# Gate loop and GEGLU kernel: residuals added by accumulating DMAs, later v loads on GpSimd's queue, one more group turned by DMA, and a new written-out order

## The chip, the cores and the metric

The kernel runs on one core of one Trainium2 chip. The metric is the device time of one execution in microseconds (us). Three runs of the kernel before took 276.53, 273.31 and 271.00 us, so its median is 273.31 us.

## The reference, cut to what matters

Part one is a complex gated linear recurrence over 768 steps for 4 batches and 8 heads of width 48. Part two is a gated feed-forward block with a gated residual over the 3072 resulting tokens of width 384.

```python
mag = np.sqrt(a_re * a_re + a_im * a_im)
scale = np.minimum(mag, 0.999) / (mag + 1e-06)
for t in range(S):
    new_re = ar * S_re - ai * S_im
    new_im = ar * S_im + ai * S_re
    S_re, S_im = new_re + k_t (outer) v_t, new_im
    y[t] = q_t @ S_re
...
g = x @ w_gate
gelu = 0.5 * g * (1.0 + erf(g * inv_sqrt2))
ffn_out = gelu * (x @ w_val) @ w_out
return x + 1.0 / (1.0 + np.exp(-(x @ w_res))) * ffn_out
```

## The kernel before, in words

The 768 steps are cut into chunks of 128. Two chunks (c = 0 and 1) of one batch make a group p; there are 12 groups, p = 4 s + b for the third s of the sequence and the batch b. A group is computed as masked attention inside a chunk, plus a state G that is carried from third to third.

Every piece of work is a named step. `Steps.add` (line 360) records it with its engine, what it reads and what it writes; the string `ORDER` (line 260) lists all steps, and the last loop of the kernel (lines 926 to 931) emits them one after the other. Each engine, and each DMA queue, therefore gets its own steps in the order of that list, and it goes through them strictly in that order: a step that has to wait holds up everything behind it on that engine. The number after a colon picks the buffer of a tile (`Y5.1:2` puts the output x of group 5, chunk 1 in x buffer 2 of 9). The words `log`, `trig` and `gelu` are loads of an activation table on ScalarE (line 929), which is on ACT. The table `eo` in `PARAMS` (line 64) says which engine does a step that more than one engine could do.

The steps of a group p, in the order of the data:

- Loads on SP's queue, 192 KB each: `Lar`, `Lai`, `Lq`, `Lk` (line 516), `Lvf` (line 880). The v data land as float32 in `vf` (2 buffers) and are cast to bfloat16 by `VC` (lines 882 and 883) on POOL, ACT or DVE.
- Gates (lines 518 to 648): squares `SQI` and `SQR`, `ADD`, logarithms and exponentials `LNR`, `EXR`, `LM`, the angle `TH` and `ATN`, all over 128x768 float32. Sums over time on PE: `CSL` (line 588) for the magnitude, followed by `EX` and `EI` on ACT; `CST` (lines 621 and 622) for the angle, followed by `OFF` and `FR`, `ABS`, `SIN` and `COS`.
- The angle of chunk 0 has to be carried to chunk 1. There are two ways. For a group in the list `cma`, one more matrix product with a constant (line 621) adds the sum over chunk 0 inside `CST p.1`. For a group that is not in the list, `CRA p` scales the last row of chunk 0 (line 670), and `CDA p`, an accumulating DMA from POOL's queue (line 675), adds it to the first row of `ai` of chunk 1; only then can `CST p.1` run. `CRB` and `CDB` are the same from third to third.
- The decay of the state over a third: the small DMAs `DR`, `DS`, `DE`, `DI`, `DT` from POOL's queue, `ML` and `ME` on ACT, `MM` and `MN`, then `EN` (line 755, scales G) and `EB` (line 760, casts it).
- Products (lines 684 to 702): `QE`, `KE`, `QR`, `KR` on DVE write padded q and k tiles. From group `turn` on, `QT` and `KT` (line 700) turn them with DMA transposes on SP's queue. For the groups before it, four `TP` steps (line 727, eight transposes each, on PE) and four `CP` copies (line 732, on DVE or ACT) do that.
- Attention (lines 704 to 799): `AT` on PE, `AM` (mask) on DVE, `DK`, `MI`, `ED` for the state, `Y` on PE, and `X`, the cast of the output to the bfloat16 tile x, on ACT or DVE. There is one PSUM tile for y.

The feed-forward block works on 8 units. Units 0 to 3 are one group each (256 tokens), units 4 to 7 are two groups each (512 tokens, four chunks jj = 0 to 3). x is turned by PE (`XT`, `XC`) for groups 0 to 4 and by DMA (`XD`, line 809) from group 5 on. Then come `GP` and `VP` (line 828, PE), `GE` (gelu, ACT), `HM` (line 839, DVE), `RP` (line 843, PE) and `SG` (ACT), `OP` (line 853, 12 products, PE), `OT` (line 858, DVE), the residual and the store `ST` (line 868, SP's queue). The residual is one of:

- `RX` (line 865): POOL or DVE adds x to the output tile before the store. All 24 chunks do this in the kernel before.
- `AX` (line 871): the tile is stored without x, and a DMA on POOL's queue then adds x to the stored rows in DRAM. It reads x and the stored output, so it waits until `ST` has landed, and the buffer of x is free only after it.

The weights (line 894) come as 12 casting DMAs on POOL's queue: `Wg0` to `Wg3`, `Wv0` to `Wv3`, `Wr`, `Wo0` to `Wo2`. `HOLDW` and `HOLDO` are one-element copies on POOL that wait for a load of `ai`, so that what stands behind them on POOL starts later.

The lines that choose between the ways:

```python
if p >= TURN:                                              # QT, KT  (699)
both = p in PARAMS["cma"] and c == 1                       # (612)
if p in PARAMS["vhw"]:                                     # Lvf + VC  (878)
    ...
else:
    st.add("LV%d.%d" % (p, c), "POOL", lambda c=c: nc.gpsimd.dma_start(out=st["v", p][:, c], in_=rows(v, p, c)), ...)   # (886)
rese = PARAMS["rese"][min(u, len(PARAMS["rese"]) - 1)] if u < NU - 1 else PARAMS["resl"]   # (861)
if rese == "DMA":
    st.add("AX%d.%d" % (u, jj), "POOL", lambda t0=t0, pc=(p, c): nc.gpsimd.dma_start(
        out=out[t0:t0 + 128, :], in_=st["x", pc], accum_op=OP.add),
        r=[("x", (p, c)), ("out", (u, jj))], w=[("out", (u, jj))])                          # (871)
```

Of the kernel before, what the change touches and what calls it, by code (L numbers as in the profile page):

```python
# [18 lines left out]
 'turn': 5,  # L19
# [39 lines left out]
 'rese': ['POOL'],  # L59
 'resl': 'POOL',  # L60
 'vhw': [0, 1, 2, 3, 4, 5, 6, 7, 8, 9, 10, 11],
 'cma': [4, 5, 6, 7, 8, 9, 10, 11],
# [50 lines left out]
        'MM7': 'DVE',  # L113
        'MM8': 'DVE',
        'MM9': 'DVE',
        'MN10': 'POOL',
        'MN11': 'DVE',
        'MN4': 'DVE',
# [4 lines left out]
        'MN9': 'DVE',  # L123
# [64 lines left out]
        'SQR10': 'DVE',  # L188
        'SQR11': 'ACT',
        'SQR2': 'ACT',  # L190
# [3 lines left out]
        'SQR6': 'ACT',  # L194
# [66 lines left out]
Lar0.1:0 log LNR0.1:0 SQR0.1 Lai0.1:0 SQI0.1:0 ADD0.1 LM0.1 EXR0.1 TH0.1 Lar0.0 Lai0.0 LNR0.0 EXR0.0 SQI0.0 TH0.0 trig  # L261
ATN0.0 CST0.0:0 SQR0.0 ATN0.1 CSL0.1:10 CST0.1:2 Lai1.1:1 Lar1.1:1 Lai3.0:2 Lai4.1:3 Lai1.0 ADD0.0 SQI1:1 log LM0.0
EI0.1 CSL0.0:3 Lar1.0 SQR1 ADD1 LM1 OFF0.1 FR0.1 ABS0.1 LNR1 EX0.1 EXR1 Lk0.0:0 TH1 Lai3.1 Lvf0.1:0 Lai5.1:4 EX0.0
EI0.0 OFF0.0 VC0.1:0 DE0:0 CRB0 HOLDO Lar3.1:2 Lk0.1 trig ATN1 FR0.0 SIN0.0:0 SIN0.1 SQI3:2 ABS0.0 COS0.0 CSL1.1:211
CST1.0:1 KE0.1 CSL1.0:3 KE0.0 CST1.1:0 Lq0.0:0 Lar3.0 SQR3 ADD3 COS0.1 KR0.0 log LNR3 KR0.1 Lar4.1:3 EX1.1 Lvf0.0:1
Lai4.0 SQI4:3 OFF1.0 OFF1.1 VC0.0 FR1.1 QE0.0 EX1.0 EXR3 DE1:1 DK0.0 QR0.0 Lar4.0 Lq1.0:1 Lai2.0:5 Lvf1.1:0 Lq0.1
EI1.0 FR1.0 ABS1 SQR4 CRB1 Lai5.0 Lar2.1:0 Lai2.1 TP0.0.1:00 TP0.0.0:11 Lq1.1 EI1.1 CP0.0.0 Lar2.0 AT0.0.0:00 LM3
QE0.1 TH3 QR0.1 AM0.0.0 ADD4 CP0.0.1 DR4:0 Lk1.0:1 QE1 TP0.1.0:31 AT0.0.1:11 trig SIN1:1 SQI2:0 ATN3 SQR2 COS1
TP0.1.1:20 AM0.0.1 Y0.0:0 CP0.1.1 Lk1.1 ADD2 log LM2 CSL3.1:100 AT0.1.1:00 CST3.1:0 CSL3.0:2 QR1 KE1 CP0.1.0
AT0.1.0:11 AM0.1.1 AM0.1.0 EI3.1 EX3.0 EI3.0 CSL2.1:311 CST3.0:2 OFF3.1 LNR4 EX3.1 MI0:0 FR3.1 X0.0 Lar5.1:1 Lvf1.0:1  # L270
Lar5.0 Wg0 Wg2 Wv3 Wg3 EI2.1 Wg1 Wv0 KR1 EX2.1 Y0.1:1 X0.1 XT0.1:10 TP1.0.0:00 XC0.1 EXR4 OFF3.0 FR3.0 VC1.0:1 Wr SQR5
XT0.0:3 CP1.0.0 XC0.0 CRB3 TP1.0.1:11 SQI5:1 LNR2 EXR2 CP1.0.1 ABS3 Wo2 Wv1 GP0.5:2 trig COS3:0 DK0.1 ED0 ADD5 VC1.1
Lk2.0:2 GP0.0:0 AT1.0.0:00 gelu GE0.0 HOLDW Lq2.0:2 GP0.2:3 Lar7.1:2 AT1.0.1:11 GP0.4:1 GE0.2 GE0.4 GE0.5 AM1.0.0
TP1.1.0:00 CP1.1.0 RP0.0:3 GP0.3:1 RP0.1:0 TH4 Lq3.0:3 Lk2.1 GP0.1:2 SG0.0 DK1.0 SG0.1 Lq2.1 Wo0 TP1.1.1:31 Lvf2.0:1
Lq3.1 GE0.1 AM1.0.1 TH2 DE2:2 GE0.3 CP1.1.1 Lk3.0:3 VP0.0:0 Y1.0:2 X1.0 AT1.1.0:00 AM1.1.0 MI1:1 VP0.5:2 CSL2.0:1 trig
ATN2 HM0.5 HM0.0 CST2.1:3 AT1.1.1:11 AM1.1.1 OFF2.1 log LNR5 EX2.0 EXR5 EI2.0 FR2.1 CST2.0:2 Y1.1:3 DK1.1 X1.1 LM4
trig ATN4 XT1.0:01 XC1.0 Wv2 OFF2.0 FR2.0 TH5 ABS2 SIN2:1 SIN3 COS2 VP0.4:3 VP0.2:0 VP0.3:1 VP0.1:2 HM0.2 HM0.3 HM0.1
HM0.4 DS4.0:0 DR5:1 Wo1 KE2 DS4.1 Lai6.0:0 KR2 QE2 ATN5 DS5.0:1 QR2 XT1.1:0 CSL4.0:111 DS5.1 OP0.0.0:2 OT0.0:0 log ML5
EI4.0 OP0.1.0:3 EX4.0 XC1.1 OT0.1:1 CRB2 TP2.0.0:10 Lai6.1 GP1.2:0 GP1.1:2 CP2.0.0 TP2.0.1:31 AT2.0.0:00 QE3 RX0.0 QR3
DI4 ED1 AM2.0.0 DE3:3 CDB0 VC2.0:2 CDB1 gelu GE1.2 GE1.1 Lvf2.1:0 Lar9.1:3 Lk3.1 VC2.1 Lai7.0:1 GP1.0:1 RP1.0:0  # L280
TP2.1.1:20 CP2.0.1 DT4.0:0 AT2.0.1:11 GP1.5:3 GE1.0 SQI6:2 SG1.0 GE1.5 CP2.1.1 AM2.0.1 DK2.0 VP1.5:1 GP1.3:0 HM1.5
MI2:0 KE3 RP1.1:2 DT4.1 RX0.1 GP1.4:3 Y2.0:4 Lvf5.0:1 VP1.0:1 X2.0 HM1.0 KR3 SG1.1 GE1.4 GE1.3 CST4.1:2 TP2.1.0:31
CSL4.1:0 VC5.0:3 Lar6.1:0 CP2.1.0 Lai11.1:2 Lar7.0 Lar6.0 CST4.0:1 AT2.1.1:00 log LM5 CSL5.0:300 EX4.1 ML4 OFF4.1
EI4.1 EI5.0 EX5.0 SQR6 SQR7 AT2.1.0:11 OFF4.0 AM2.1.1 FR4.1 CSL5.1:0 Lk4.0:0 XT2.0:20 CST5.1:3 DI5 MM4:0 AM2.1.0 FR4.0
EX5.1 EI5.1 OFF5.1 XC2.0 Y2.1:5 VP1.3:1 Lai7.1 ABS4 ADD6 SQI7:0 TP3.0.1:20 X2.1 VP1.4:0 HM1.3 FR5.1 HM1.4 Lk4.1 ST0.0
Lq5.0:0 Lvf6.1:0 ME4 LNR6 DR6:0 ADD7 MN4 EN4 TP3.0.0:11 CST5.0:3 CP3.0.0 VC6.1:0 VP1.1:0 DR7:1 OFF5.0 CP3.0.1 FR5.0
VP1.2:1 HM1.1 XT2.1:3 AT3.0.1:00 HM1.2 TP3.1.0:20 AT3.0.0:11 LM6 LNR7 EXR6 ME5 EXR7 Lvf3.0:1 Lar9.0 Lar10.0:1 Lvf3.1:0
# [3 lines left out]
AT3.1.0:01 SQR9 SG2.0 GP2.5:1 GE2.0 SG2.1 QE4 QR4 X3.0 AM3.1.0 GE2.5 GP2.1:3 GE2.1 VP2.0:2 DS7.0:0 DT5.1:1 CRB5 DT5.0
RX1.0 Lvf4.1:0 VP2.3:0 VP2.4:1 Lq7.0:2 Y3.1:7 HM2.0 XT3.0:31 TP4.0.0:20 HM2.3 Lai9.0 HM2.4 CP4.0.0 ST0.1 VP2.5:0 Lk5.0
HM2.5 XC3.0 Lai8.1 RX1.1 VC4.0:2 CRB4 Lar10.1 EB4:0 DE5:4 trig ATN6 VP2.1:1 TP4.0.1:21 COS5 X3.1 SQI9:1 DS7.1 HM2.1
CP4.0.1 DE4:5 XT3.1:0 Lvf8.0:1 ST1.0 AT4.0.0:10 CSL6.0:311 VC4.1 ATN7 log LM7 ML7 Lar8.1:0 AT4.0.1:01 Lar8.0 DK4.0
# [667 lines left out]
```

## Time and profile before

| | |
|---|---|
| runs | 271.00, 273.31, 276.53 us (median 273.31) |
| the profiled execution | 271.58 us, of which its trace spans 269.8 us |
| PE busy in the span | 236.5 us (88%) |
| DVE busy | 225.6 us (84%) |
| ACT busy | 204.8 us (76%), 43.6 us of it 34 table loads |
| POOL busy | 86.6 us (32%) |
| DMA | q1 (SP's queue) 68.7%, q0 (POOL's queue) 10.8% of the 16 engines' span |

One execution is profiled. An engine's busy time is the union of its instructions. PE's matrix products overlap one another, so what one costs in a row of them is read from the chain of waits (six products of 512 columns: 1.30 us), and not from the mean duration of one. The chain of waits is the work that ended last, followed back from the end: at each step to what released it, or to the instruction before it on the same engine. "SPq" and "POOLq" are the instruction queues that issue DMAs.

### The profile page before, as it was taken

What the parts mean: (1) busy time and instruction counts of PE and PEld (TensorE: products, weight loads), DVE (VectorE), ACT (ScalarE), POOL (GpSimd) and SP (SyncE); (2) the same over time, 40 slices, a digit from 0 to 9 for tenths busy, and PEclk for the clock granted to TensorE, in tenths of its full rate; (3) what the DMA queues carried; (4) which work ended last, traced back from release to release, by engine and by line L of the source; (5) the groups of instructions that cost most, each with busy time, mean ns of one, the idle gap of its engine ahead of it and who ended that gap; (6) DMA issues with size and microseconds to landing.
All of it is one profiled execution on the core that took longest, in us unless ns stands there. A gap on an engine that the chain in (4) does not pass through costs nothing.

```text
span 269.8 us, 5300 instructions
## 1 busy us (share of the span) xinstructions
PE 236.5 (88%) x1931; PEld 149.8 (56%) x1942; DVE 225.6 (84%) x379; ACT 204.8 (76%) x327; POOL 86.6 (32%) x136
## 2 busy tenths in 40 slices
PE   0536495788989999999999999999999999999993
PEld 0213354566766777686754556645566445654461
DVE  1678989799998999998999998998978899724743
ACT  4889999799959998998999986776958846234420
POOL 4030193302631376355923153461254000310000
PEclk9986569999999999999999999999999999999999
DMA  7999999999999399999599879867954383220112
GB/s 145 201 203 211 201 186 185 184 185 189 201 179 209 58 197 188 195 207 196 84 185 213 187 168 142 192 131 167 225 124 62 101 177 95 61 87 1 61 58 87
DMA packets 170458, 41.34 MB, mean 153 GB/s; under 512 B 162368, under 2 KB 170432, under 8 KB 170432
## 3 DMA queue, kind: packets, MB, share of 16 engines
q1 hardware_dynamic: 163200, 37.04, 68.7%
q0 software_dynamic: 7232, 3.96, 10.8%
q8 instruction: 15, 0.25, 0.4%
q14 instruction: 11, 0.09, 0.1%
HBM read 31.33 MB, written 4.76 MB: 134 GB/s over the span
## 4 chain that ended last, share of the span: by engine, by line
PE 66%; DVE 10%; DMA 9%; ACT 6%; SPq 3%; issue 2%; POOL 2%; DVEq 0%
PE gv L828 27%; PE sums L853 16%; DMA wr<-in_moe_w_res_dram 5%; PE sums L622 5%; PE sums L588 4%; PE sums L843 3%; SPq L516 3%; PE at L739 3%; PE sums L621 2%; ACT L929 2%; PE y L787 2%; DMA ar<-in_a_re_dram 1%; PE y L790 1%; DMA vf<-in_v_dram 1%; ACT ar L500 1%
## 5 line engine op out<-in xcount | busy, mean ns | idle before, releaser
L500 ACT ACTIVATE h<-gv 128x512 bf16<-128x512 f32 x72 | 41.1, 598 | 19.5 <-PE gv L828 18.5
L828 PE MATMUL gv<-xT,wv 128*128 128x256 bf16 (+1 forms) x282 | 54.1, 324 | 2.0 <-DMA wv<-in_moe_w_val_dram 1.2
L839 DVE SCALAR_TENSOR_TENSOR h<-h,gv 128x512 bf16<-128x512 bf16 x72 | 47.3, 679 | 10.0 <-PE gv L828 9.2
L828 PE MATMUL gv<-xT,wg 128*128 128x256 bf16 (+1 forms) x283 | 53.7, 325 | 1.5 <-DVE xT L511 1.0
L853 PE MATMUL sums<-wo,h 128*128 128x384 bf16 x288 | 49.4, 326 | 0.0
L929 ACT ACT_TABLE_LOAD x34 | 43.6, 1283 | 1.3 <-PEq L946 0.7
L828 PEld LDWEIGHTS <-wv 128*128 128x128 bf16 x288 | 27.1, 97 | 19.6 <-issue 2.1
L828 PEld LDWEIGHTS <-wg 128*128 128x128 bf16 x288 | 27.2, 98 | 19.3 <-DMA wg<-in_moe_w_gate_dram 1.3
L853 PEld LDWEIGHTS <-h 128*128 128x128 bf16 x288 | 27.6, 98 | 18.0 <-issue 0.7
L742 DVE TENSOR_TENSOR atm<-at,mask 128x512 bf16<-128x512 f32 x48 | 32.0, 681 | 3.5 <-PE at L739 3.4
L500 ACT ACTIVATE ar<-ar 128x768 f32<-128x768 f32 x29 | 24.1, 845 | 0.1
L500 ACT ACTIVATE sg<-sums 128x384 f32<-128x384 f32 x24 | 11.7, 491 | 14.7 <-PE sums L843 14.0
L858 DVE SCALAR_TENSOR_TENSOR ot<-sg,sums 128x384 f32<-128x384 f32 x24 | 13.0, 547 | 11.6 <-PE sums L853 9.3
L622 PE MATMUL sums<-ai,ut 128*128 128x384 f32 x40 | 18.7, 552 | 0.3 <-ACT ai L500 0.3
L576 POOL DMA_DIRECT2D m<-d x16 | 11.4, 727 | 20.1 <-DMA d<-m 8.7
L511 POOL CAST v<-vf 128x384 bf16<-128x384 f32 x15 | 9.8, 654 | 24.5 <-DMA vf<-in_v_dram 24.5
L622 PE MATMUL sums<-ai,lt 128*128 128x384 f32 x8 | 5.1, 727 | 13.6 <-ACT ai L500 13.6
L500 ACT ACTIVATE m<-m 96x8 f32<-96x8 f32 (+2 forms) x29 | 13.4, 471 | 4.1 <-DMA m<-d 2.2
L843 PE MATMUL sums<-wr,xT 128*128 128x384 bf16 x72 | 15.0, 326 | 0.2 <-DMA wr<-in_moe_w_res_dram 0.2
L865 POOL TENSOR_TENSOR ot<-ot,x 128x384 f32<-128x384 f32 x10 | 12.0, 1198 | 8.7 <-DVE ot L858 8.6
L787 PE MATMUL y<-v,atm 128*128 128x48 bf16 x192 | 12.5, 185 | 1.5 <-DVE x L511 1.0
L787 PEld LDWEIGHTS <-atm 128*128 128x128 bf16 x192 | 11.1, 97 | 4.5 <-DVE x L511 1.6
(94 smaller groups left out, 455.6 us busy)
## 6 DMA issues: line engine op xcount, KB each, us to landing
ar<-in_a_re_dram SPq DMA_DIRECT2D x24, 192.0 KB, 4.0
ai<-in_a_im_dram SPq DMA_DIRECT2D x24, 192.0 KB, 3.9
k<-in_k_dram SPq DMA_DIRECT2D x24, 192.0 KB, 3.8
vf<-in_v_dram SPq DMA_DIRECT2D x24, 192.0 KB, 4.1
q<-in_q_dram SPq DMA_DIRECT2D x24, 192.0 KB, 4.0
out_dram<-ot SPq DMA_DIRECT2D x24, 192.0 KB, 2.5
wg<-in_moe_w_gate_dram POOLq DMA_DIRECT2D x4, 288.0 KB, 8.7
wv<-in_moe_w_val_dram POOLq DMA_DIRECT2D x4, 288.0 KB, 14.1
```

The costliest lines, as they stand in the source:

```text
L500: return nc.scalar.activation(out=out, in_=in_, func=func, **kw)
L576: st.add("DS%d.%d" % (p, u), "POOL", lambda u=u: nc.gpsimd.dma_start(out=st["m1", p][u * D:(u + 1) * D], in_=st["d1", p].rearrange("r (h d ...
L622: return r + [nc.tensor.matmul(out=o, lhsT=tmat[c if s == 0 else 1], rhs=part(("ai", p), (c,)), start=not both, stop=True)]
L742: st.add("AM" + sfx, "DVE", lambda: nc.vector.tensor_tensor(out=st["atm", i], in0=st["at", i], in1=mask4, op=OP.mult), r=[("at", i)], w=[( ...
L787: r.append(nc.tensor.matmul(out=ys, lhsT=st["atm", (p, c, hg)][:, j], rhs=st["v", p][:, c, h], start=True, stop=first))
L828: st.add("%sP%d.%d" % (nm.upper(), u, f), "PE", lambda f=f, fs=fs, nm=nm, w=w: [nc.tensor.matmul(out=st[nm + "p", (u, f)][:, j * 256:j * 2 ...
L839: st.add("HM%d.%d" % (u, f), "DVE", lambda f=f, h2=h2: nc.vector.scalar_tensor_tensor(out=h2(), in0=h2(), scalar=0.5, in1=gv(("vp", (u, f) ...
L843: st.add("RP%d.%d" % (u, jj), "PE", lambda jj=jj: [nc.tensor.matmul(out=st["rp", (u, jj)], lhsT=st["xT", u][:, i, jj * 128:(jj + 1) * 128] ...
L853: st.add("OP%d.%d.%d" % (u, jj, hh), "PE", lambda jj=jj, fs=fs: [nc.tensor.matmul(out=st["op", (u, jj)], lhsT=st["h2", u][:, f, jj * 128:( ...
L858: st.add("OT%d.%d" % (u, jj), "DVE", lambda jj=jj: nc.vector.scalar_tensor_tensor(out=st["ot", (u, jj)], in0=st["sg", u][:, jj], scalar=1. ...
L865: st.add("RX%d.%d" % (u, jj), rese, lambda jj=jj, pc=(p, c), eng=eng: eng.tensor_tensor(out=st["ot", (u, jj)], in0=st["ot", (u, jj)], in1= ...
L929: nc.scalar.preload_act_table_set(tables[nm])
```

## The change

Four switches and the order are changed; no line of the functions is.

- `rese` goes from POOL to DMA: the 20 chunks of units 0 to 6 get `AX` in place of `RX`. Unit 7 keeps `RX` (two on POOL, two on DVE).
- `vhw` loses groups 6 to 11: for them 12 `LV` (a casting DMA on POOL's queue straight into the bfloat16 tile) stand in place of 12 `Lvf` on SP's queue and 12 `VC` (8 on POOL, 3 on ACT, 1 on DVE).
- `turn` goes from 5 to 4: group 4 loses 4 `TP` and 4 `CP` and gets `QT4` and `KT4` on SP's queue.
- `cma` loses groups 8 to 11 (this is in the diff, though not in the short title): the four products of line 621 with their loads go, and 4 `CRA` (2 POOL, 2 DVE) and 4 `CDA` on POOL's queue come.
- `eo` gives other engines to many of the remaining steps.
- `ORDER` is written anew, from 1355 to 1348 entries. It has 37 table loads instead of 34.

```diff
- 'turn': 5,
+ 'turn': 4,
...
- 'rese': ['POOL'],
+ 'rese': ['DMA'],
  'resl': 'POOL',
- 'vhw': [0, 1, 2, 3, 4, 5, 6, 7, 8, 9, 10, 11],
- 'cma': [4, 5, 6, 7, 8, 9, 10, 11],
+ 'vhw': [0, 1, 2, 3, 4, 5],
+ 'cma': [4, 5, 6, 7],
...
+        'CRA10': 'POOL',
+        'CRA11': 'POOL',
+        'CRA8': 'DVE',
+        'CRA9': 'DVE',
...
-        'RX6.0': 'POOL',
-        'RX6.1': 'DVE',
-        'RX6.2': 'DVE',
-        'RX6.3': 'POOL',
-        'RX7.0': 'DVE',
+        'RX7.0': 'POOL',
         'RX7.1': 'DVE',
         'RX7.2': 'DVE',
-        'RX7.3': 'DVE',
+        'RX7.3': 'POOL',
```

How many of the steps that can change engine stand where, before and after:

| steps | before | after |
|---|---|---|
| RX | 14 DVE, 10 POOL | 2 DVE, 2 POOL |
| VC | 15 POOL, 5 DVE, 4 ACT | 10 POOL, 2 DVE |
| CP | 15 DVE, 5 ACT | 13 DVE, 3 ACT |
| X | 14 ACT, 10 DVE | 17 ACT, 7 DVE |
| XC | 2 ACT, 8 DVE | 8 ACT, 2 DVE |
| OFF | 13 ACT, 11 DVE | 9 ACT, 15 DVE |
| SQR | 7 ACT, 6 DVE | 5 ACT, 8 DVE |
| CRB | 5 DVE, 3 POOL | 2 DVE, 3 POOL, 3 ACT |
| EN, EB | 8 DVE, 8 POOL | 1 DVE, 12 POOL, 3 ACT |
| MM, MN | 8 DVE, 8 POOL | 3 DVE, 13 POOL |

The start of POOL's queue (its own steps of `ORDER`, in their order) before and after:

```
before: VC0.1 DE0 HOLDO DE1 DR4 Wg0 Wg2 Wv3 Wg3 Wg1 Wv0 Wr Wo2 Wv1 HOLDW Wo0 DE2 Wv2 DS4.0 DR5 Wo1 DS4.1 DS5.0 DS5.1 DI4 DE3 CDB0 VC2.0 ...
after:  VC0.1 Wv0 DE1 HOLDW HOLDO DE0 VC0.0 Wg0 DE3 Wv3 LV6.1 Wg1 Wg2 VC1.0 Wv1 Wg3 Wr Wv2 VC1.1 Wo2 Wo0 Wo1 DR5 DR4 DE2 CDB1 DS4.0 DS4.1 CDB0 VC2.0 ...
```

The start of SP's queue:

```
before: Lar0.1 Lai0.1 Lar0.0 Lai0.0 Lai1.1 Lar1.1 Lai3.0 Lai4.1 Lai1.0 Lar1.0 Lk0.0 Lai3.1 Lvf0.1 ...
after:  Lar0.0 Lai0.0 Lar0.1 Lai0.1 Lar1.1 Lai1.1 Lar1.0 Lai1.0 Lar5.0 Lar3.0 Lai3.0 Lar2.1 Lai2.0 ...
```

The end of the new order:

```diff
+RP7.2:2 VP7.5:0 ST6.0 ST6.2 GP7.1:3 HM7.5 VP7.0:1 HM7.0 VP7.1:0 AX6.2 GE7.1 RP7.3:3 RP7.1:1 SG7.3 SG7.1 SG7.2 HM7.1
+OP7.0.0:0 OT7.0:0 RX7.0 AX6.3 AX6.0 ST7.0 ST6.1 OP7.3.0:3 OT7.3:1 RX7.3 OP7.1.0:1 AX6.1 ST7.3 OT7.1:2 RX7.1 OP7.2.0:2
+OT7.2:0 ST7.1 RX7.2 ST7.2
```

More of the change, by code (lines that the diff above doesn't have):

```diff
@@ L112 @@
         'MM6': 'POOL',
[L113 to L118, printed above, removed]
+        'MM7': 'POOL',
+        'MM8': 'POOL',
+        'MM9': 'POOL',
+        'MN10': 'DVE',
+        'MN11': 'POOL',
+        'MN4': 'POOL',
         'MN5': 'POOL',
@@ L122 @@
         'MN8': 'POOL',
-        'MN9': 'DVE',
+        'MN9': 'POOL',
         'OFF0.0': 'DVE',
@@ L187 @@
         'SQR1': 'DVE',
[L188 to L190 removed]
+        'SQR10': 'ACT',
+        'SQR11': 'DVE',
+        'SQR2': 'DVE',
         'SQR3': 'DVE',
@@ L193 @@
         'SQR5': 'ACT',
-        'SQR6': 'ACT',
+        'SQR6': 'DVE',
         'SQR7': 'ACT',
@@ L271 @@
[L271 to L275, printed above, removed]
@@ L291 @@
[L291 to L294, printed above, removed]
-Lvf5.1:0 QE5 AM4.0.1 ADD9 XC3.1 LNR9 EI6.0 EXR9 QR5 EX6.0 MM5:1 OP2.0.0:2 OT2.0:1 KE5 OP2.1.0:1 CSL7.0:000 EI7.0 EX7.0
```

301 lines of the change are left out of this document (138 added, 163 removed).

## The prediction

> **What bounds the kernel now.** First the slices of the page (its part 2), to see who is full when.
>
> ```profile
> PE   0536495788989999999999999999999999999993
> DVE  1678989799998999998999998998978899724743
> ACT  4889999799959998998999986776958846234420
> DMA  7999999999999399999599879867954383220112
> ```
>
> A slice is 6.7 us. PE is full from about slice 10 to the end; before that ACT, DVE and the DMA engines are full and PE has holes. Next the busy times by stage. I cut at 69 us, where unit 0's last OP ends (the chain has that OP end at 69.05), and at 265.5, where PE ends.
>
> ```profile
> 0.00:69.00 69.00, 43.08 (x324) 28.33 (x324) 55.09 (x98) 60.48 (x88) 19.61 (x38) 0.88 1.10 189
> 69.00:140.00 71.00, 68.48 (x706) 51.49 (x706) 69.20 (x114) 65.09 (x106) 37.67 (x56) 1.00 0.94 171
> 140.00:200.00 60.00, 59.67 (x444) 33.63 (x447) 55.63 (x92) 48.40 (x82) 21.86 (x31) 1.00 0.85 171
> 200.00:265.50 65.50, 65.23 (x463) 36.34 (x465) 44.53 (x76) 30.85 (x53) 7.43 (x11) 1.00 0.32 80
> ```
>
> The columns are stage, length, then busy PE, PEld, DVE, ACT, POOL, granted clock, DMA share, GB/s. PE idles 25.9 us in the first stage, 2.5 in the second, 0.6 in the other two together. So from 69 us on the time is PE's work and little else; between 69 and 140 DVE (69.2 of 71) is as full as PE. Third, the chain of waits.
>
> ```profile
> 33.20 1.56 POOL wg L900 x2
> ...
> 37.77 13.90 DMA wr<-in_moe_w_res_dram
> ...
> 80.86 0.45 PE tp L727 x8
> ...
> 84.68 0.77 PE sums L621 x2
> ```
>
> The first stage hangs on gates and weights: seven weights were issued from 33.2 on, and the seventh, wr, landed at 51.7. The last two lines price what the change takes from PE: 0.45 us a TP step, 0.65 to 0.77 a line 621 product. Last the groups and issues that price the rest.
>
> ```profile
> L865 POOL TENSOR_TENSOR ot<-ot,x 128x384 f32<-128x384 f32 x10 | 12.0, 1198 | 8.7 <-DVE ot L858 8.6
> L865 DVE TENSOR_TENSOR ot<-ot,x 128x384 f32<-128x384 f32 x14 | 7.8, 572 | 0.1
> L675 POOL DMA_DIRECT2D ai<-G x8 | 7.0, 872 | 12.9 <-ACT ai L500 12.9
> L602 POOL DMA_DIRECT2D m<-d x16 | 12.7, 793 | 2.8 <-DMA d<-Ei 2.4 <-issue 0.3
> out_dram<-ot SPq DMA_DIRECT2D x24, 192.0 KB, 2.5
> wr<-in_moe_w_res_dram POOLq DMA_DIRECT2D x1, 288.0 KB, 13.9
> ai<-G POOLq DMA_DIRECT2D x8, 1.5 KB, 3.6
> QT<-padQ SPq DMA_TRANSPOSE x7, 4.1
> ```
>
> In the first four the numbers behind the bar are busy us, mean ns of one and idle before; in the last four the last number is us from issue to landing.
>
> **The sum** is made against the profiled execution, 271.58 us (span 269.8 and 1.8 around it). That is 0.6% under the median of 273.31.
>
> Group 4 by DMA: 4 TP at 0.45 leave PE, -1.8 us. They stood after 100 us (the TP's last records are in the stage 100 to 130), where PE is dense, so the whole counts. In place come QT4 and KT4 on SP's queue, about 1.85 us of issue each (median of the seven QT), landing 4.1 us after issue. Behind QT4 the order leaves 3.3 us of PE work before AT4.0.0 (RP2.0, VP2.1, CSL6.0 and so on by their chain prices): late by 0.8. Their DMA time is added at a share of 0.94; SP loses 12 loads further on, and the stage that follows has a share of 0.85.
>
> Groups 8 to 11 without the constant product: 4 x 0.70 (mean of the pieces in the chain), -2.8, all in the dense stages. They take on CRA, CDA and a landing of 3.6 before CST p.1. The order leaves 11.2, 3.3, 3.5 and 6.0 us of PE work there for groups 8 to 11: short by 0.4 in all.
>
> Residuals: 12 RX leave DVE (12 x 0.572 = 6.9), 8 leave POOL (9.6). 20 AX come to POOL at 0.87 of issue (nearest row: the accumulating ai<-G), 17.4. An AX waits on POOL until its store has landed, 2.5 after issue. Only four have under 3 us of PE work between ST and AX (AX4.3 none, AX3.0 1.7, AX6.2 2.0, AX1.0 2.5), so POOL stands some 4 us in all; behind AX4.3 stand CDB6 and MN8, both used over 5 us later, and it is hidden. An AX also holds x: its landing is not in this trace. Bounds: 2.5 (a plain store) and 13.9 (a 288 KB casting DMA amid full DMA engines). I take 3.6, the accumulating row, since most AX run where the share is 0.85 or less. The tightest reuses of x have 4.2 (AX1.1 to X5.0), 4.3 (AX5.1 to X11.0), 4.6 (AX1.0 to X6.1), 6.2, 6.3 and 7.1 us of PE work between: nothing lost at 3.6, and 0.3 granted for SP's queue being late.
>
> v: 12 VC go (8 POOL, 3 ACT, 1 DVE); 12 LV come on POOL at about 0.79 (the m<-d row, the POOL DMA with the most elements), 9.5 in all. The same bytes are read. The closest LV (LV7.0) is 6.7 us of PE work ahead of its use, against a vf landing of 4.1: free. If it landed as late as wr, 7 us would be lost once.
>
> Engines: counting every step at its row's mean, DVE loses 13.6 us (RX 6.9, XC 2.1, EN and EB 3.5, others), 4.8 of them before unit 3's OP. ACT gains 2.9 (3 table loads at 1.28 are 3.8, less smaller moves), but up to unit 3's OP it is level (-0.2), and later ACT has room (48.4 of 60, 30.9 of 65.5). POOL gains 24 on 87 of 270. So the added ACT and POOL time costs nothing while their steps are not late. Of PE's 2.5 idle between 69 and 140, which mostly follows DVE, I take half back: -1.2 (bounds 0 and -2.5).
>
> The front: up to unit 0's second OP the row sums are level (PE 35.6 against 35.8, ACT 66.4 against 65.8, DVE 61.4 against 61.3). The new order puts unit 0's last GE behind 10.9 us more ACT work (row means, less the 0.1 by which its instructions overlap) and the attention of group 1 ahead of unit 0, so I put the first OP at 66 instead of 65.15: +0.8 (bounds -3, four loads fewer ahead of it at about 1 us each less LV6.1, and +6, below).
>
> The tail: after PE's end OT, RX and the store take 4.3 us, unchanged. AX6.1 is new there: ST6.1 stands behind ST7.0 on SP and is issued about 2.7 us before PE's end, lands 2.5 later, then POOL issues (0.87) and 3.6 pass: 4.3 or more. Level with the last store; +0.5 (bounds 0 and +3).
>
> Waits in all 0.8 + 0.4 + 0.3 = 1.5. Sum: 271.58 - 1.8 - 2.8 - 1.2 + 0.8 + 1.5 + 0.5 = 268.6 us.
>
> A rule that speaks against the change: the Trainium skill, "SBUF — State Buffer", section "SBUF: two separate sides", says that GpSimd can't write the descriptors of its DMAs while a VectorE operation in a two-port mode holds the shared port, so that such a DMA stalls. The rows before do not show it: with DVE 97% busy (69 to 140), POOL's small DMAs land in 2.7 to 3.7 us, SP's loads in 3.8 to 4.1. By the rule the 36 DMAs added to POOL would land later, which is the mechanism of the second rival.
>
> **Rivals.** (1) Weights late. Ten of the twelve weights now stand behind DE3 on POOL, which waits for EX3.1 on ACT (40.55 before, and the ACT work ahead of it is within 1 us of that): they start at about 41.5 instead of 33.2, +8.3. Wv0 and Wg0 go earlier, -5.2 (seven weights in 18.5 us: 2.6 each), and LV6.1 stands between them, up to +2.6. OP0 then starts 5.7 later than the sum has it at worst: 274.3. Against it: SP's Lvf2.0 must wait for VC1.0, which stands behind Wg2, so SP leaves the DMA engines to the weights, and a weight should then take less than 2.6.
>
> (2) Slower: AX holds x. If an AX lands 7.7 us after issue, the six reuses are late by 3.5, 3.4, 3.1, 1.5, 1.4 and 0.6, 13.5 us; with one y tile in PSUM a late X stops the next Y on PE. That gives 282.1. At 5.4 us of landing it eats 3 us and the kernel is level with the profiled execution; from 7.2 on it is slower by over 2%. For it: every DMA that carries over 200 KB from POOL took 8.7 to 15.8 us. Against it: those came in a burst at a share over 1.1.
>
> (3) The front gets shorter. If the DMA engines and not ACT set it, the four loads less give -3 in place of +0.8, and DVE's lighter load returns all 2.5 instead of 1.2, without new waits: 268.6 - 3.8 - 1.3 - 1.5 = 262.0.
>
> **How the numbers follow.** Forecast 0.42, own range 264.5 to 272.5; weights late 0.17; AX holds x 0.25; short front 0.16. Two per cent, about what a measurement of this kernel can tell from no change, is 267.8 or 278.8 against the median. Of the forecast's 0.42 I put 0.17 below 267.8. Faster: 0.17 + 0.16 = 0.33. Slower: 0.25 and 0.02 of the weights, 0.27. Same: 0.40. The range goes from 262 (half of the short front is out, 0.08) to 282 (half of the AX case, 0.12).
>
> **What would show it.** PE busy down by 4.6; line 727 with 128 records instead of 160 and line 621 with 8 instead of 16; PE idle between unit 0's OP and the end about 3 us. AX landing (out_dram<-x) near 3.6: right; over 7 with waits of X or Y behind it: rival 2. PE waiting on weights before OP0, with wg issued at 41: rival 1. The forecast is wrong if PE's idle after 69 us grows past 7, or if unit 0's second OP ends later than 72 or earlier than 66.

## The result and the profile after

The changed kernel takes 287.67 us (median; 287.56, 287.00, 287.78 and 295.53), the kernel before 273.31: a ratio of 1.055, 95% interval 1.046 to 1.063. The medians in this document are of all executions, the ratios and their intervals only of those within 1.5% of the fastest of their kernel, so the two need not agree to the last digit. The profiled execution took 287.56 us, its trace spans 285.8 (269.8 before), 16.0 us more. In its rows a line number is 32 lower than in the code above: at L707 is line 739 (`AT`), L668 is 700 (`QT`, `KT`), L836 is 868 (`ST`), L839 is 871 (`AX`). In rows of the other kernels the distance differs, and the names of the tiles tell which step it is.

The slices of the page after (7.1 us each), the answer to those shown of before:

```profile
PE   0735677689999998973999799996999999999991
DVE  2759998769998998881799698876799789713712
ACT  6899899499899999891599679977477765225210
DMA  7999999999999999999639999989977858831036
```

PE has holes in the dense part that it did not have (the 7 and 3 in the 18th and 19th slice, the 7 in the 23rd, the 6 in the 28th), and the DMA engines are full up to the 19th without a gap and again from the 22nd to the 29th. The same by stage, with the columns of before (length, PE, PEld, DVE, ACT, POOL, granted clock, DMA share, GB/s):

```profile
0.00:69.00 69.00, 42.62 (x295) 27.84 (x296) 52.48 (x88) 59.31 (x88) 19.98 (x40) 0.88 1.11 187
69.00:140.00 71.00, 62.90 (x620) 47.31 (x618) 58.33 (x93) 58.39 (x96) 36.53 (x51) 0.95 1.09 190
140.00:200.00 60.00, 54.70 (x414) 31.37 (x413) 50.36 (x80) 51.09 (x82) 35.87 (x48) 1.00 0.96 160
200.00:270.00 70.00, 70.00 (x525) 38.73 (x523) 49.51 (x81) 37.81 (x65) 21.66 (x28) 1.00 0.62 108
```

Between 69 and 140 us PE idles 8.1 us instead of 2.5, between 140 and 200 it idles 5.3 instead of 0.3; no other engine took over, for DVE fell from 69.2 to 58.3. In the same stage the granted clock fell from 1.00 to 0.95. What rose is the DMA share: 0.94 to 1.09, 0.85 to 0.96, 0.32 to 0.62. What PE waits for (us in total, times, longest):

```profile
PE sums L590 <- ACT ai L468: 10.9, 2, 7.0
PE at L707 <- DMA QT<-padQ: 9.2, 3, 6.5
PE tp L695 <- DVE padQ L663: 4.1, 1, 4.1
...
PE at L707 <- DMA KT<-padK: 2.9, 2, 2.4
```

The first and third are in the front, where before had 13.9 and 2.4 of their kind. New are 12.1 us in which `AT` waits for DMA transposes; before had none. The longest, 6.53 us at `AT5`, can be followed on SP's queue (start, us, instruction):

```profile
121.31 3.92 SPq L668 DMA_TRANSPOSE KT<-padK  x1
125.27 0.58 SPq L836 DMA_DIRECT2D out_dram<-ot  x1
125.95 3.50 SPq L668 DMA_TRANSPOSE QT<-padQ  x1
```

`KR5` and `QR5` were ready at 119.4 and 121.9, but the queue reached `QT5` at 125.95, issued it for 3.50 us, and it landed at about 133.1. Issue times of 1.3 to 2.6 us for a `QT` before had become 1.6 to 3.9. The DMA queues and landings (last number: us from issue to landing):

```profile
q1 hardware_dynamic: 154880, 35.73, 64.3%
q0 software_dynamic: 22720, 9.08, 27.0%
...
out_dram<-ot SPq DMA_DIRECT2D x24, 192.0 KB, 3.5
out_dram<-x POOLq DMA_DIRECT2D x20, 192.0 KB, 4.5
...
xT<-x SPq DMA_TRANSPOSE x14, 3.6
KT<-padK SPq DMA_TRANSPOSE x8, 5.5
QT<-padQ SPq DMA_TRANSPOSE x8, 6.1
```

Stores landed in 2.5 us before, `QT` in 4.1. No engine waits for an AX to land in this trace. POOL's queue took 10.8% of the 16 engines' 269.8 us before, 29.1 us; now 27.0% of 285.8, 77.2 us.

By place the 16.0 us of these two profiled executions are: 4.5 in the front (unit 0's first OP starts at 69.65, before at 65.15), 9.4 from there to PE's end (200.35 us long before, 209.8 now), 2.1 in the tail (PE's end to the span's end).

### The profile page after: what moved, and what is told of

The parts are those of the page before. It is cut to its first block, busy times and chain, and to the rows that moved or that the text cites. A ratio compares the mean times of both kernels' runs of the same rounds, so it can differ in the third digit from the quotient of the medians.

```text
span 285.8 us, 5222 instructions
## 1 busy us (share of the span) xinstructions
PE 239.6 (84%) x1902; PEld 150.6 (53%) x1902; DVE 215.3 (75%) x346; ACT 208.0 (73%) x333; POOL 118.5 (41%) x170
## 3 DMA queue, kind: packets, MB, share of 16 engines
q1 hardware_dynamic: 154880, 35.73, 64.3%
## 5 line engine op out<-in xcount | busy, mean ns | idle before, releaser
L807 DVE SCALAR_TENSOR_TENSOR h<-h,gv 128x512 bf16<-128x512 bf16 x72 | 47.3, 681 | 19.8 <-PE gv L796 13.4
L796 PE MATMUL gv<-xT,wg 128*128 128x256 bf16 (+1 forms) x288 | 55.2, 334 | 3.2 <-DMA wg<-in_moe_w_gate_dram 2.2
L796 PE MATMUL gv<-xT,wv 128*128 128x256 bf16 (+1 forms) x288 | 56.4, 335 | 0.3 <-ACT sg L468 0.3
L839 POOL DMA_DIRECT2D out_dram<-x x20 | 19.5, 1021 | 39.9 <-DMA out_dram<-ot 39.9
L479 POOL CAST v<-vf 128x384 bf16<-128x384 f32 x10 | 7.9, 787 | 35.7 <-DMA vf<-in_v_dram 35.6
L468 ACT ACTIVATE ar<-ar 128x768 f32<-128x768 f32 x27 | 22.3, 844 | 0.1
L707 PE MATMUL at<-QT,KT 96*128 96x128 bf16 x128 | 10.7, 224 | 12.1 <-DMA QT<-padQ 9.2
L643 POOL DMA_DIRECT2D ai<-G x12 | 11.3, 938 | 15.7 <-ACT ai L468 10.7
L570 POOL DMA_DIRECT2D m<-d x16 | 15.3, 977 | 5.6 <-DMA d<-Ei 5.6
L707 PEld LDWEIGHTS <-KT 96*128 96x128 bf16 x128 | 8.6, 100 | 15.2 <-issue 8.5
L544 POOL DMA_DIRECT2D m<-d x16 | 12.7, 813 | 8.7 <-DMA d<-m 7.8
L468 ACT ACTIVATE Ei<-sums 128x384 f32<-128x384 f32 x24 | 11.6, 491 | 6.3 <-PE sums L556 6.1
```

Source lines behind the costliest of these rows:

```text
L468: return nc.scalar.activation(out=out, in_=in_, func=func, **kw)
L544: st.add("DS%d.%d" % (p, u), "POOL", lambda u=u: nc.gpsimd.dma_start(out=st["m1", p][u * D:(u + 1) * D], in_=st["d1", p].rearrange("r (h d ...
L570: st.add("DT%d.%d" % (p, u), "POOL", lambda u=u: nc.gpsimd.dma_start(out=st["m3", p][u * D:(u + 1) * D].rearrange("p r h -> p (r h)"), in_ ...
L707: return [nc.tensor.matmul(out=st["at", i][:, j], lhsT=lhs("K", c, hg * 4 + j), rhs=lhs("Q", c, hg * 4 + j), start=True, stop=True) for j ...
L796: st.add("%sP%d.%d" % (nm.upper(), u, f), "PE", lambda f=f, fs=fs, nm=nm, w=w: [nc.tensor.matmul(out=st[nm + "p", (u, f)][:, j * 256:j * 2 ...
L807: st.add("HM%d.%d" % (u, f), "DVE", lambda f=f, h2=h2: nc.vector.scalar_tensor_tensor(out=h2(), in0=h2(), scalar=0.5, in1=gv(("vp", (u, f) ...
```

## The experiments

Each was timed beside the kernel before, whose medians there were 271.8 to 272.6 us. Three theories: T, the DMA time that the parts add fills the 16 engines, so that SP's transposes land late; O, the new order places transposes, weights and a store badly; P, POOL, waiting for stores ahead of each AX, holds up the chain of the state. Where a ratio to before has no interval, the lowest and highest run are given.

Below, "DMA time" is a queue's share of the page times the span: us of all 16 engines. It is no fixed price of a transfer. For q0 it repeats well (76.7 to 78.5 us in the six kernels of the new order that have all AX and LV). For q1 it does not: in the twelve kernels, the changed one among them, whose q1 carries 154,880 packets it is 177.4 to 188.0 us.

### One part at a time in the order of before

LV alone (before_lv): `vhw` without groups 6 to 11, each `VC` and its `Lvf` replaced by an `LV` some 6 us of PE work earlier.

> The kernel before with one part of the change: 12 LV in place of 12 Lvf and 12 VC of groups 6 to 11, each about 6 us of PE work ahead of where its VC stood; order and engines otherwise as before. Theory T: 12 LV cost more DMA time than 12 Lvf and come into the dense stage, 275 to 280 us, q0 up by 5% of the span or more. Theory O: 270 to 274 us, as VC leaves the engines.

272.10 us, ratio 1.002 (0.999 to 1.004): what O expected, and T missed by 3 us or more. LV is free there, although 12 LV take 23.7 us of DMA time on q0 (52.8 less 29.1) where 12 Lvf took 12.8 on q1 (185.4 less 172.6).

AX alone (before_ax), each 2 to 4 us of PE work behind its store; two stores are moved up besides, so that x is read before its buffer is used again:

```diff
- 'rese': ['POOL'],
+ 'rese': ['DMA'],
...
-RX0.0 ... RX6.3
+AX0.0 ... AX6.3
```

> The kernel before with one part of the change: 20 AX in place of the 20 RX of units 0 to 6, each 2 to 4 us of PE work behind its store; ST3.1 and ST5.2 moved up to their OT, since x must be read before its buffer is used again; order and engines otherwise as before. Theory T: AX adds DMA time where the share is 0.85 to 0.94, so slower than before: 276 to 281 us. Theory O: DVE loses 6.9 us and nothing else happens: 270 to 273 us. Theory P: POOL stands behind each store for 2 to 3 us, 20 times, and holds DS, DT and VC: 277 to 283 us, with waits of PE for G and v, not for QT.

280.98 us (275.5 to 284.4). Two cases of waiting stand out in its trace, that of the execution of 281.17 us: POOL waits 51.7 us for stores, and PE waits 4.5 us at 247 us for an `XD` whose x came late because the buffer was held by an AX (ACT stood 3.8 us for that AX to land). That looked like P and like the second rival, so the data were taken out of it (before_ax_one_row):

```diff
-    out=out[t0:t0 + 128, :], in_=st["x", pc], accum_op=OP.add),
+    out=out[t0:t0 + 1, :], in_=st["x", pc][0:1], accum_op=OP.add),
```

> The kernel before with AX in the same places as in the run of AX alone (281.0 us), but each of one row of 128, so that x is left out of the other rows. T (the DMA time of AX's data): 272 to 274.5 us. P and rival 2 (POOL waits for stores, x is held until AX has landed): these waits stay, 278 to 281 us.

271.67 us, ratio 0.998 (0.995 to 1.001): the whole price is gone. POOL's waits for stores, first with whole data, then with one row:

```profile
POOL out_dram L852 <- DMA out_dram<-ot: 51.7, 9, 23.4
```

```profile
POOL out_dram L852 <- DMA out_dram<-ot: 50.2, 9, 20.2
```

They are nearly the same, and cost nothing. So P falls, and what AX costs comes with its data: 9.3 us by the medians (281.0 less 271.7), 3.8 by the lowest of the four runs of before_ax, which still lies above all ten with one row (270.4 to 273.1). How the data cost it is less clear than T has it. With one row an AX landed in 3.1 us, with whole data in 4.3, and the stores in 2.2 and 2.9; ACT's wait for the held x was 1.3 us instead of 3.8, and PE's wait of 4.5 us for `XD` was 0.8. So a large part of the loss in this execution is a held x, the second rival's mechanism, brought on by data that landed later.

Group 4 by DMA beside LV (before_lv_turn4): `turn` 4, `TP4` and `CP4` out, `KT4` right behind `KR4`, `QT4` right behind `QR4`.

> The kernel before with two of the parts in its own order: the 12 LV for Lvf and VC in groups 6 to 11, and group 4 turned by DMA (KT4 right behind KR4, QT4 right behind QR4). No AX, all of cma, order and engines of before. If the new order is what costs (O), the parts cost nothing here: 269.5 to 273 us, PE busy about 1.8 us less, and QT4 waits under 0.5 us at AT4. If a DMA transpose costs more than the PE work that it replaces, 274 us or more with a wait of PE at line at<-qk for QT. Theory P (POOL's waits on stores) expects no loss here, since there is no AX.

279.85 us, ratio 1.032 (1.027 to 1.037), against 272.10 without it: the opposite of my 1.0 us gain, by 7.8 us. SP's queue:

```profile
87.72 0.81 SPq L499 DMA_DIRECT2D k<-in_k_dram  x1
98.00 1.86 SPq L683 DMA_TRANSPOSE KT<-padK  x1
99.97 0.51 SPq L499 DMA_DIRECT2D ai<-in_a_im_dram  x1
```

From 88.5 to 98.0 SP issues nothing: it stands at `KT4` until DVE has written padK, with loads behind it. Two of them could have gone at once: in the next kernel they are issued at 90.27 and 91.23. (before_turn4_later) puts `KT4` behind four of these loads:

```diff
-KR4 KT4:1 AT3.1.1:10 ... Lai8.0:5 Lq4.0 Lvf4.0:1 Lai9.1:3 ... QR4 QT4:1
+KR4 AT3.1.1:10 ... Lai8.0:5 Lq4.0 Lvf4.0:1 Lai9.1:3 ... QR4 KT4:1 QT4:1
```

> The kernel before with LV and group 4 turned by DMA as in the run that took 279.9 us, but KT4 stands just ahead of QT4 and so behind four loads that it held up: SP stood for 9.4 us at KT4 until KR4 was done, and 3.7 at QT4. If SP standing is the price, 272 to 275 us; if it is the DMA time of two transposes in a full stretch, 278 to 281 us.

276.62 us, ratio 1.017 (1.012 to 1.023), between the two expectations: 3.2 us came back with the loads that SP had held up, 4.5 us remain, 1.8 of PE work saved notwithstanding. Against before_lv q1's DMA time is 4.8 us more with `KT4` early and 6.6 with it late (172.6, 177.4 and 179.2 us); whether that is what remains was not taken apart further.

### Parts undone in the new order

(after_rx) RX back for all AX, just ahead of the store; (after_lvf) Lvf and VC back for LV.

> The changed kernel with one part undone: RX on the engines (as in the kernel before) in place of the 20 AX, each RX just ahead of its store; all else as changed. Theory T (DMA time): the DMAs added to POOL's queue fill the DMA engines (q0 went from 10.8% of 269.8 us to 27.0% of 285.8 us, 29 to 77 us), the transposes land later (QT 4.1 to 6.1 us) and PE waits for them (12 us). Then this run is clearly faster than the changed kernel: 278 to 283 us, q0 near 16%, PE's waits for QT and KT below 7 us. Theory O (order): the new order puts transposes, weights and one store late on their queues, and the parts by themselves cost nothing: 285 to 289 us, waits for QT and KT as before this edit. A third, P (POOL waits on stores, 39.9 us in all, and holds the state's chain): 280 to 284 with QT and KT still near 6 us.

> The changed kernel with another part undone: v of groups 6 to 11 loaded by SP's queue and cast by the engines, as in the kernel before, in place of the 12 LV; VC stands where LV stood and the load about 40 entries ahead of it; all else as changed. Theory T: 12 LV are part of the 48 us of added q0 time; the same bytes on SP's queue cost about 12 us of DMA time, so this run is 279 to 284 us with q0 near 20%. Theory O: 286 to 290 us (VC comes back to the engines, SP gets 12 more loads in front of its transposes).

294.68 us, ratio 1.080 (1.073 to 1.087), and 292.75, 1.074 (1.069 to 1.079): both slower than the change whole and outside every range expected. They tell little of AX and LV, since the steps that came back had no place in this order: in after_rx POOL waited 34.4 us for `OT`, ahead of its RX. The next kernels take work out and put none in.

(after_no_ax) the 20 AX entries dropped, x left out; (after_ax_one_row) the one-row edit shown above; (after_ax_plain) the same bytes without the addition, which overwrites the feed-forward result of these rows:

```diff
-    out=out[t0:t0 + 128, :], in_=st["x", pc], accum_op=OP.add),
+    out=out[t0:t0 + 128, :], in_=st["x", pc]),
```

> The changed kernel without the 20 AX; nothing takes their place, so x is left out of the output rows of units 0 to 6, POOL waits for no store, x buffers are free early and q0 carries only weights, LV and small DMAs. T and P both expect a gain: 280 to 283 us, with the DMA transposes of q and k landing in 4.7 us or less instead of 5.5 and 6.1. O (place in the queues, not AX) expects 286 to 288.5 us, since the wait of 6.5 us at AT5, the front and the tail stay.

> The changed kernel with every AX cut to one row of 128: the same DMA in the same place, which waits for the same store and holds the same x buffer, but moves 768 bytes instead of 96 KB; x is left out of the other 127 rows. T: the time falls as it does without AX at all (280 to 283 us). P: POOL's waits on stores are what AX costs, so the time stays at 286 to 289 us although q0's share of the DMA engines falls by about 9%. O: 286 to 288.5 us in both.

> The changed kernel with AX as a plain casting copy of x into the output rows, so that it overwrites them: the same bytes read from x and written, the same waits, no accumulation. If the accumulation (reading the rows back and adding) is what takes the DMA engines' time, 280 to 284 us and q0's share 2% or more below 27.0%; if it is the bytes and the cast, 286 to 289 us with q0 at 26.5 to 27.5%.

| kernel | us | ratio | q0 DMA time |
|---|---|---|---|
| change | 287.67 | 1.055 (1.046 to 1.063) | 77.2 |
| AX a plain copy | 280.65 | none (runs 275.2 to 281.7 us) | 71.9 |
| AX of one row | 278.33 | 1.019 (1.012 to 1.025) | 55.8 |
| no AX | 276.48 | 1.007 (1.003 to 1.012) | 53.4 |

All steps of AX kept and only its data gone: 9.3 us less (POOL's waits ahead of AX 40.3 us in all, 39.9 in the change). That it is the same 9.3 as in the order of before is chance: there the runs scatter by 9 us, and the loss has another place. POOL's time, the waits and x buffers are worth the 1.9 us between the last two rows. Without AX, PE's wait at `AT5` is 3.3 us instead of 6.5, and `QT` lands in 4.8 us instead of 6.1. An AX takes (77.2 - 53.4) / 20 = 1.19 us of DMA time, as a plain copy 0.93, and its issue on POOL is 0.95 us against 0.58 as a copy. So the addition costs too, 7.0 us by the medians (5.4 to 12.6 between the nearest and the farthest runs, 295.53 left out); the copy's price over no AX is within its own scatter. T as stated, DMA engines that are full, doesn't explain that: the copy takes 18.5 of AX's 23.8 us of DMA time, q0's share fell by 1.3% and not by the 2% expected, and between 69 and 140 us the engines are as full as with the addition:

```profile
69.00:140.00 71.00, 63.51 (x643) 48.36 (x642) 59.60 (x94) 58.29 (x98) 35.31 (x51) 0.95 1.12 186
```

From 200 us on the share is lower, 0.49 instead of 0.62. Why the addition costs so much beyond its share is open.

(after_no_early_ax) drops only the 8 AX of units 0 to 3:

> The changed kernel without the 8 AX of units 0 to 3; the 12 of units 4 to 6 stay, and x is left out of the output rows of units 0 to 3. If AX costs where the DMA engines are full (share 1.09 from 69 to 140 us, 0.96 to 200), most of the 11.2 us goes with these 8: 278.5 to 281.5 us. If each AX costs the same or the late ones cost by the tail, 283 to 286 us.

280.31 us (277.2 to 287.4, so one run takes as long as the change). By the medians the 8 early AX cost 7.4 us, 0.9 each, the 12 late ones the 3.8 above no AX, 0.3 each: most of the price falls where the DMA share is 0.96 to 1.09.

(after_turn5) group 4 by PE again, (after_cma_all) the constant product for groups 8 to 11 again:

> The changed kernel with group 4 turned by PE again (4 TP and 4 CP back, KT4 and QT4 gone from SP's queue). By my sum alone it would be 1.8 us slower, 289 to 290 us. If a DMA transpose's real price is that SP waits for its input, and with it the loads behind it, as in the kernel before with turn 4 (279.9 against 272.1 us), then it is faster, 281 to 285 us.

> The changed kernel with groups 8 to 11 in cma again: four products of line 590's kind back on PE, CRA and CDA of these groups gone from POOL and its queue. By my sum (2.8 us of PE work against 0.4 of waits) it would be 2 to 3 us slower, 289 to 291 us. If POOL's queue, where CDA waits for CRA behind AX and LV, is on the path, it is 284 to 287 us.

282.19 us, ratio 1.036 (1.030 to 1.043): 5.5 us faster, with 1.8 us more work on PE. q1's DMA time fell from 183.8 to 178.6 us, 2.6 for each of the two transposes, against 1.07 for an Lvf; but that is within the scatter of q1 given above. And, for the constant product, 285.87 us, 1.050 (1.043 to 1.057): PE is busy 1.7 us more and the time is not longer; the intervals overlap, so no gain is shown either.

### Moves in the new order

(after_weights_first) only moves `DE3` on POOL behind `Wo1`, which frees the weights from waiting for ACT. (after_turn5_first) only moves seven entries of SP's queue:

```diff
-... CSL6.0:100 Lq8.1:2 Lk11.1:1 ... Lar10.0:0 ... Lk6.0 ... KR5 ST2.0 Lk8.0 KT5:1 ... ST2.1 ... QR5 OFF6.0 QT5:1 FR6.0
+... CSL6.0:100 ... KR5 KT5:1 ... QR5 OFF6.0 QT5:1 Lq8.1:2 Lk11.1:1 Lar10.0:0 Lk6.0 ST2.0 Lk8.0 ST2.1 FR6.0
```

(after_three_moves) does both, and puts `ST6.1` right behind `ST6.0`.

> The changed kernel with one step moved: DE3, on POOL's queue, stands behind Wo1, so that wg is issued at about 33 us and not behind EX3.1 at 41.4. O: unit 0's OP starts at 66 to 67 us and not at 69.65, and the end comes by as much earlier, 283.5 to 285.5 us. If the front is made up for by a later wait (AT5 waits for a DMA transpose whose place on SP's queue is unchanged), the end stays at 286.5 to 289 us. T expects no change but the front's, since DMA traffic is the same.

> The changed kernel with seven entries of SP's queue (Lq8.1, Lk11.1, Lar10.0, Lk6.0, ST2.0, Lk8.0, ST2.1) moved from ahead of QT5 to behind it, so that KT5 and QT5 are issued 3 to 4 us earlier. O: PE's wait of 6.5 us at AT5 falls below 2 us, and the end comes 4 to 6 us earlier, 281.5 to 284 us. T: the transposes land as late as before, because the DMA engines are full (share 1.09), the wait stays above 4 us and the time stays within 1.5 us of 287.6. P: no change in POOL's waits, and none in time.

> The changed kernel with both moves above and a third: ST6.1 stands right behind ST6.0 on SP's queue and not behind ST7.0. O: front -3.5, hole at AT5 -5, tail -2, in sum 276 to 279 us. T and P expect that the DMA time and POOL's waits on stores stay, and more of it shows up as new holes: 281 us or more.

Weights first: 293.26 us, ratio 1.079 (1.074 to 1.084), slower by 5.6, and unit 0's first OP starts at 77.67. The weights were issued from 31.3 on, next to the gate loads; the load of `ai` issued at 40.60 took 4.29 us to issue, and ACT stood for it:

```profile
54.87 0.84 ACT L468 ACTIVATE m<-ai 128x768 f32<-128x768 f32 x1 [9.65 <-DMA ai<-in_a_im_dram]
```

So the wait of `DE3` protects the gates, and O is false at this place. The kernel before issues its weights from 33.2 on too, but its queue has no `ai` load between 27 and 65 us. Transposes first: 285.13 us, 1.048 (1.042 to 1.054). PE's wait at `AT5` fell from 6.5 to 1.8 us, but only 2.5 us of it came back (the intervals overlap): new waits appeared behind it, 2.1 us for v at 139.8 and 4.0 for `QT` at 159.9. That trace is of its longest execution, 289.51 us, so it shows where waits can come up and not what they cost in the others. Both theories missed a part: O the time (281.5 to 284), T the wait (above 4 us). The three together, which O put at 276 to 279 us: 292.62, 1.078 (1.072 to 1.084); from `AT11` to the end they took 37.2 us against 38.6, which is `ST6.1`'s share of the tail.

### The parts together

(after_undone) RX on DVE right behind `OT`, group 4 by PE and `cma` whole, in the new order:

> The changed kernel's order with three parts undone: RX on DVE right behind OT for the 20 AX, group 4 turned by PE, cma for groups 4 to 11; LV stays. By the single runs 287.7 - 11.2 - 5.5 - 1.8 = 269.2 us, plus what 20 additions of about 0.69 us on DVE cost where DVE is not waiting: 269 to 273 us. If the new order is bad in itself (theory O), it stays above 276 us.

286.84 us, ratio 1.051 (1.044 to 1.058): the single gains do not add up. It is 10.4 us above no AX (276.48). The products and transposes that came back are 4.6 us of PE work by the prices of the chain; what makes the other 5.8, the 20 additions on DVE or their place, was not taken apart. By the test set for it the result speaks for O: with the DMA share back at 0.94 and 0.87 from 69 to 140 and 140 to 200 us, the new order with these steps in it is still 15 us slower than the old one. In its trace PE waits 4.95 us at 156.5 for a `QT` that was issued at 148.39, as soon as its input was written, and took 8.1 us to land (the DMA share was 1.90 between 151 and 154 us), so a stage's mean share can hide a full stretch. (after_one_row_turn5) has AX of one row and group 4 by PE:

> The changed kernel with AX of one row (x is left out of the other 127) and group 4 turned by PE. If group 4's DMA transposes make up the rest beside AX's data, 278.3 - 5.5 = 272 to 274 us. If they cost only because AX fills the DMA engines, or the rest is the new order, the PE work of 1.8 us comes on top or nothing changes: 277 to 281 us.

275.63 us, ratio 1.016 (1.011 to 1.021), between the two ranges: 2.7 us under one row alone (the intervals overlap, so this gain is not shown by itself), and 4.0 above the same one-row AX in the order of before (271.67). With group 4 turned by PE, then, AX's data cost 6.6 us (282.19 less 275.63); with it turned by DMA 9.3. No version here is faster than the kernel before.

## Why the prediction was wrong

The forecast of 268.6 us failed, and by its range too. Step by step:

- **Residuals by DMA.** This is the step that decided. I priced an AX by its issue on POOL (0.87; measured 0.95), by its landing (3.6; measured 4.5) and by the reuse of x ("nothing lost at 3.6"). These prices were near: with one row in each AX, waits and held x cost 0 in the old order and 1.9 us in the new one. I gave no price to the DMA time of its data: 1.19 us of 16 engines each, 23.8 in all, put into stages that I had shown at a share of 0.94 and 0.85. Their data cost 9.3 us in the new order (6.6 with group 4 turned by PE) and 3.8 to 9.3 in the old one. The DMA time names the term, not its size: as a plain copy the same bytes cost 7.0 us less. The second rival had the right part and side, and 282.1 us. Its mechanism, x held until AX has landed, is seen once in before_ax, where AX landed in 3.2 to 6.6 us; in the changed kernel nothing waits for an AX to land.
- **Group 4 by DMA, -1.8 and +0.8.** The PE work fell as said (records of the line from 160 to 128). "Their DMA time is added at a share of 0.94" was left without a number, and SP standing at a transpose was not priced at all. Measured: +5.5 us in the new order (+2.7, not clear of the noise, once AX's data are gone), +7.8 and +4.5 in the old one, so 3.2 of it is the place of `KT4`. The DMA time of the two transposes is not settled: q1 has 4.8, 6.6 and 5.2 us more with them in three pairs of kernels, and 2.0 less in the fourth (178.0 with them against 180.0 without, both with AX of one row).
- **Groups 8 to 11 without the constant product, -2.8.** The PE work went (1.7 us in busy time), and no gain in time is shown; PE, with 13.4 us of idle time after 69 us, was no longer all that set the end.
- **v by LV, free.** Right in the old order (272.10 against 271.8). Its 10.9 us of extra DMA time (23.7 less 12.8) did add to the load of the new one; what that cost was not shown, since after_lvf tells little.
- **The front, +0.8.** OP0 came at 69.65, in eleven other kernels with this order of the front at 66.4 to 69.7 (median 67.3), in five with the old one at 64.0 to 65.8 (median 64.9): some 2.4 us, inside my bounds. The first rival's sign is there (behind `DE3` the weights are issued from 41.42 on, and PE waits 2.2 us for wg, 0.2 before), but its cure is not: weights ahead of `DE3` make the front 8 us longer.
- **DVE's lighter load, -1.2.** DVE did fall, by 10.3 us, and PE did not gain; the 2.5 us of idle time became 8.1 for another reason.
- **The tail, +0.5.** Measured 2.1. Not AX6.1's landing, which came 3.5 us after its issue at 279.87, ahead of the last store's: from `AT11` on, 1.9 us go without AX and 1.4 with `ST6.1` placed earlier. `ST6.1` stands on SP behind `ST7.0`, which waits for `RX7.0` on POOL, so `OT7.1` waits for its buffer until 279.46.

In sum, the change stands 16.0 us above the old order with one-row AX (271.67, the time of the kernel before). Taking both out, AX's data and group 4's transposes give back 12.0 (to 275.63). How the 12.0 divide depends on which goes first: 9.3 and 2.7, or 5.5 for the transposes and then 6.6 for the data. And 4.0 are left for the new order, its engines, LV and `cma` in it, with the front's 2.4 among them. How these 4.0 are shared out stays open.

The signs named in advance told it: PE's idle time after 69 us grew past 7 (13.4), and unit 0's second OP ended later than 72 (73.55). AX landed in 4.5 us, nearer to the forecast's 3.6 than to the second rival's 7. "PE busy down by 4.6" misled: the records of lines 727 and 621 fell as said, to 128 and 8, yet PE's busy time rose from 236.5 to 239.6 us, where the granted clock was lower behind holes (0.95 between 69 and 140 us; more below).

The row to start from is the DMA share by stage. The Trainium skill, "Trainium Kernel Development and Optimization", section "Key Constraints", says that DMAs from SP, ACT and POOL run on the same 16 engines and that issuing from several saves only issue time. The traces agree: in the seven kernels of the new order with all AX on POOL's queue the `QT` on SP's queue land in 4.8 to 6.1 us (median 5.7), in the five without AX's data in 4.6 to 5.1 (median 4.9). The rule that the prediction weighed (the Trainium skill, "SBUF — State Buffer", section "SBUF: two separate sides") is not seen to cost: with DVE busy 69.2 of 71 us between 69 and 140 in before_lv, the five LV of that stage landed in 4.6 us and LV was free. It isn't put to a hard test either, since the traces don't show which of DVE's operations ran in a two-port mode. The landings that the prediction set beside that rule are medians of the whole span; between 69 and 140 us alone they are 2.7 to 4.3 us for POOL's small DMAs and 3.9 to 4.4 for SP's loads.

## What to carry to other kernels

Set every DMA that a change adds, whatever queue issues it, against the DMA share of the stage that it goes to, before its landing and issue times. That tells where to look, not yet what it costs: here 10.9 us more of DMA time were free (LV), 18.5 were within the scatter (the plain copies), and 23.8 cost 11 (AX). An addition by DMA was dearer than the same copy, so price it by a run of its own. A transpose on the load queue also costs the time that the queue stands for its input, so look at what is queued behind it. When a resource is full, undoing one part shows the price at that state only, and gains measured one at a time need not add up.

## What the runs showed of the hardware

A hole in PE's work can cost more than its length, since the granted clock can fall behind it. The changed kernel around the wait at `AT5` (columns as above; the clock is the third number from the end):

```profile
127.00:130.00 3.00, 0.00 (x0) 0.10 (x1) 0.32 (x1) 2.81 (x6) 2.86 (x4) 1.00 1.25 179
130.00:133.00 3.00, 0.00 (x0) 0.00 (x0) 0.00 (x0) 0.00 (x0) 0.00 (x0) 0.75 1.93 219
133.00:136.00 3.00, 2.83 (x14) 1.85 (x13) 1.29 (x2) 0.40 (x2) 0.00 (x0) 0.50 1.21 234
136.00:139.00 3.00, 3.00 (x37) 2.41 (x36) 2.07 (x3) 1.76 (x3) 0.99 (x2) 0.61 1.20 221
139.00:142.00 3.00, 3.00 (x31) 2.44 (x30) 3.00 (x6) 1.35 (x3) 0.00 (x0) 1.00 0.20 41
```

For six us behind a hole of 6.5 PE is busy at a clock of 0.50 and 0.61. If its work goes in proportion to the clock, that is about 2.7 us more, an estimate of 3 x 0.50 + 3 x 0.39. The Trainium skill, "TensorE: Matmul & The Clock Gate", section "HAM oscillation — how this bites in real kernels", warns of idle gaps of PE over about 3.4 us. The hole of 6.5 us agrees, but shorter ones had a fall behind them too, here to 0.72 and 0.71 behind 3.27 us (without AX):

```profile
127.00:130.00 3.00, 2.78 (x18) 1.96 (x18) 1.37 (x3) 2.12 (x5) 0.45 (x2) 0.72 1.71 149
130.00:133.00 3.00, 3.00 (x45) 2.62 (x44) 2.63 (x5) 0.81 (x1) 0.69 (x2) 0.71 1.20 203
```

In after_turn5_first it fell to 0.50 (128 to 130 us) behind a hole of 1.84 us at 126.36, and without AX it stayed at 1.00 behind one of 2.43 us at 152.86. So in these traces the length of a hole alone doesn't decide.

DMA time in us of all 16 engines, from queue shares times spans, each from one pair of kernels: an LV 1.98, an AX 1.19 and 0.93 without the addition, an AX of one row 0.12. On q1 such a difference is less certain, by the scatter named above: a 192 KB load 1.07 (0.7 between after_lvf and the change), a transpose of q or k about 2.6 where the pairs agree. By the bytes counted, a transpose moved 0.52 MB (35.73 less 34.68, halved), a load 0.20 MB.
